# Scores of the first eight head pairs as native float32 products, two heads on 64 rows each

## The chip, the cores and the metric

The kernel runs on one core of a Trainium2 chip. The metric is the device time of one execution in microseconds (us): 705.78 us, the median of three runs (705.69 to 705.79).

## The reference, cut to what matters

```python
# q, k, v: (4, 12, 448, 64) float32; cap = 30; w_in: (768, 2048), w_out: (2048, 768) float64
scores = (1 / sqrt(64)) * matmul(q, k.transpose(0, 1, 3, 2))
scores = cap * tanh(scores / cap)
scores = scores - max(scores, axis=-1)
attn = exp(scores) / (sum(exp(scores), axis=-1) + 1e-09)
x = matmul(attn, v)              # then (4, 448, 12*64) -> (1792, 768)
h = x @ w_in
out = (h - tanh(h)) @ w_out      # (1792, 768)
```

## The kernel before, in words

Attention is worked per pair: head p and head p+6 of one batch, 24 pairs in all. Keys lie on the partitions of a score tile, in blocks of 128 (three full blocks and a tail of 64 per head; the tails of the two heads share one block), and the 448 queries lie along the free axis. A score tile goes through tanh (scale 1/(8 cap) put in beforehand), an exponential with scale cap, and then as moving operand into the product with v, which has columns of ones beside it for the sums (`pv`, L880 to L885). `numerators` and `normalize` divide. The expert layers follow: `first` (L1213 to L1215) and `second` (L1266) are products in three parts, high times high, high times low and low times high, in the one-pass type float32r; weights arrive as 64-bit floats and are decoded on VectorE (L1067 to L1081). Work of the layers for batch 0 is woven into the attention of batch 1, and so on.

The order on each engine is written out by a planner (`Plan.schedule`). Every operation is declared with an engine, an estimated cost, dependencies, buffers by tag and a due time; a list scheduler simulates all engines with these costs and fixes one order for each. "AD" operations (`copy`, L448 on ScalarE, L450 on VectorE) may go to either engine. So a changed cost or buffer changes the order of everything behind it. `SCORES` and `GROUP` are such costs.

Scores come in three kinds of work. Pairs 0 to 7 (`TILED_PAIRS`) are the tiled ones. For them `prep_pair` turns k and q with a VectorE transpose (L552), splits k into a float32r high part (a copy) and a low part (`split`, L459), copies the tails of both parts into `kt`, and makes the scaled q high on ScalarE (L575) and q low on VectorE (L580). `qk_group` (L736) then issues, for each full block, three products for each of the two heads, head 0 on rows 0 to 63 and head 1 on rows 64 to 127 of the array, the heads taken in turn: six 64-row products a group, three groups a pair. The tail block is three 128-row products with `kt`. ScalarE's tanh (L746) reads the result. Later pairs use 128-row stacks (`stack_pair`, L701) and are as they were. Pairs 0 to 10 (`F32_PAIRS`) multiply v in native float32 (L880), the others in float32r.

Of the kernel before, what the change touches and what calls it, by code (L numbers as in the profile page):

```python
# [58 lines left out]
COLS = {256: 118.0, 384: 175.5, 448: 204.0, 512: 233.0}  # L59
SCORE, FULL32 = COLS[448], 750.0  # L60

GROUP = 3 * SCORE + 400.0
SCORES = 3 * GROUP + 3 * SCORE

SHIFT = 110.0

# [248 lines left out]
class Build:  # L315
# [6 lines left out]
    def __init__(self, ctx, tc, q, k, v, w_in, w_out, out, consts, checks, general):  # L322
        self.tc, self.nc = tc, tc.nc
        nc = self.nc
        self.q, self.k, self.v, self.w_in, self.w_out, self.out = q, k, v, w_in, w_out, out
        self.general = general
        self.absc, self.s8 = consts
        self.B, self.H, self.S, self.D = q.shape
        self.NP = self.H // 2
        self.DM, self.DFF = w_in.shape  # L330
        self.ND = self.DM // 128
        self.NF = self.DFF // 128
        self.FULL = self.S // 128 * 128
        self.TAIL = self.S - self.FULL
        B, S, D = self.B, self.S, self.D
        nm = self.nm = "g" if general else "f"
        self.cst = ctx.enter_context(tc.tile_pool(name=nm + "cst", bufs=1))
        self.sb = ctx.enter_context(tc.tile_pool(name=nm + "sb", bufs=2))
        self.ps = ctx.enter_context(tc.tile_pool(name=nm + "ps", bufs=1, space=PSUM))
        self.dram = ctx.enter_context(tc.tile_pool(name=nm + "dram", bufs=1, space=bass.MemoryType.DRAM))  # L340
        self.u_kept = [self.dram.tile([128, 2, self.DM], F32, name=f"{nm}uk{f}") for f in range(self.NF)]
        self.uid = 0
        self.plan = Plan(self.make)
        for name, n in self.sizes().items():
            self.plan.tag(name, n)

        self.fixed = {"kst": [], "kz": [], "kt": [], "vraw": []}  # L350
        S = self.S
        for i in range(self.plan.tags["kst"]):
            t = self.cst.tile([128, 2 * S + self.TAIL], F32R, name=f"{nm}kst{i}")
            nc.gpsimd.memset(t.bitcast(F32)[:, S : S + self.TAIL], 0.0)
            self.fixed["kst"].append(t)


        for i in range(self.plan.tags["kz"]):
            t = self.cst.tile([128, 2 * S], F32R, name=f"{nm}kz{i}")
            nc.gpsimd.memset(t.bitcast(F32)[D:, 0:S], 0.0)  # L360
            nc.gpsimd.memset(t.bitcast(F32)[:D, S:], 0.0)
            self.fixed["kz"].append(t)
        for i in range(self.plan.tags["kt"]):
            t = self.cst.tile([128, 2, 2, self.TAIL], F32R, name=f"{nm}kt{i}")
            nc.gpsimd.memset(t.bitcast(F32)[:D, :, 1, :], 0.0)
            nc.gpsimd.memset(t.bitcast(F32)[D:, :, 0, :], 0.0)
            self.fixed["kt"].append(t)
        self.v1s = {F32: [], F32R: []}
        for i in range(self.plan.tags["vraw"]):
            t = self.cst.tile([128, 4, 2, D], F32, name=f"{nm}vraw{i}")  # L370
            self.fixed["vraw"].append(t)
        tail = B * self.TAIL
        self.xt = [self.cst.tile([128, tail], F32, name=f"{nm}xt{d}") for d in range(self.ND)]
        self.x, self.xt_ops = {}, {d: [] for d in range(self.ND)}
        self.raw_qk, self.ready, self.raw_v = {}, {}, {}
        self.raw, self.u, self.w, self.kept_op = {}, {}, {}, {}
        self.segments = [(m, a, z) for m, a, z in SEGMENTS]
        later = {m for m, a, _ in self.segments if a}
        self.x_kept = {
            m: [self.dram.tile([128, 2, self.FULL], F32, name=f"{nm}xk{m}_{d}") for d in range(self.ND)] for m in later  # L380
        }
        self.y_kept = {
            m: [self.dram.tile([128, self.DM], F32, name=f"{nm}yk{m}_{i}") for i in range(3)] for m in later
        }
        self.x_ops, self.y_ops = {}, {}
        self.acc = {}
        self.at = 0.0
        if not general:
            self.least, self.flagf, self.flag = checks
            self.seen = self.cst.tile([128, 2, self.NF], F32, name="seen")  # L390
            self.ok = self.cst.tile([128, 2, self.NF], F32, name="ok")
            self.bad = self.cst.tile([128, 2], F32, name="bad")
            self.seen_ops = []

    def sizes(self):
        g = self.general
        n = dict(kraw=2, qraw=2, kT=1, qT=1, kst=2, kz=1, ql=1, kt=1, qst=2, vraw=1, v1=3, v2=2, e=2, eh=4, el=3)
        n.update(num=1, sumT=1, r14=2, rb=1, x=self.NP, xh=self.ND, xl=self.ND, w64=2, u=2, wi=2, wo=3)
        n.update(g=1, gh=1, gl=1, o=3, s=2, h=1, acc0=1, acc1=1, acc2=1, acc3=1, acc4=1)
        if g:  # L400
# [140 lines left out]
    def prep_pair(self, b, p):  # L541

        nc, S, D, F, TL, plan = self.nc, self.S, self.D, self.FULL, self.TAIL, self.plan
        T, tr = {}, {}
        for nm in ("k", "q"):
            raw, j, ops = self.raw_qk.pop((nm, b, p))
            t = T[nm] = plan.buf(nm + "T", [128, S])
            tr[nm] = self.dve(  # L550
                S,
                lambda t=t, raw=raw, j=j: nc.vector.transpose(t(), raw()[:, j].rearrange("p j a -> p (j a)")),  # L552
                ops, [t], [raw],
            )
        if not self.tiled(b, p):
            return self.stack_pair(b, p, T, tr)
        kst, kt, qst = plan.buf("kst"), plan.buf("kt"), plan.buf("qst", [128, 2, S], F32R)
        kops = list(
            self.split(
                S, lambda: kst()[:, :S], lambda: kst()[:, S + TL :], T["k"], [tr["k"]], ([kst], []),  # L560
                ([T["k"]], [kst, T["k"]]),
            )
        )
        tops = []
        for h, c0 in ((0, F), (1, 0)):
            rows = slice(D * h, D * h + D)
            tops.append(
                self.copy(
                    2 * TL, lambda h=h, rows=rows: kt()[rows, :, h, :],
                    lambda rows=rows, c0=c0: self.pieces(kst(), rows, c0), kops,  # L570
                    [] if h else [kt], [kst, kt] if h else [kst],
                )
            )
        o1 = self.act(
            S, lambda: nc.scalar.activation(qst()[:, 0, :], T["q"](), AF.Copy, scale=self.s8), [tr["q"]],  # L575
            [qst], [T["q"]], aps=1,
        )
        o2 = self.dve(
            S,
            lambda: nc.vector.scalar_tensor_tensor(  # L580
                qst()[:, 1, :], T["q"](), self.s8, qst()[:, 0, :].bitcast(F32), op0=ALU.mult, op1=ALU.subtract
            ),
            [o1], [], [qst, T["q"]], extra=60,
        )
        self.ready[b, p] = dict(kst=kst, kt=kt, qst=qst, kops=kops, tops=tops, qops=[o1, o2])

    def tiled(self, b, p):
        return b * self.NP + p < TILED_PAIRS

    def pieces(self, kst, rows, c0):  # L590

        S, TL = self.S, self.TAIL
        t = kst[rows, c0 : c0 + S + 2 * TL].bitcast(F32)
        return t.rearrange("p (a b) -> p a b", b=TL)[:, 0 : S // TL + 2 : S // TL + 1, :]

    def stack_pair(self, b, p, T, tr):

# [113 lines left out]
        )  # L711
        return [t], cost

    PRODUCTS = ((0, 0), (0, 1), (1, 0))

    def qk_group(self, b, p, c, dsts, e):

        nc, S, D = self.nc, self.S, self.D
# [5 lines left out]
        ps = self.s_banks(b, p, heads)  # L724

        def fn():
            qst = r["qst"]()
            for n, (i, j) in enumerate(self.PRODUCTS):
                for h in range(heads):
                    rows = slice(D * h, D * h + D) if heads == 2 else slice(0, 2 * D)  # L730
                    c0 = 128 * c + self.TAIL * h
                    if heads == 2:
                        k = r["kst"]()[rows, (S + self.TAIL) * i + c0 : (S + self.TAIL) * i + c0 + 128]
                    else:
                        k = r["kt"]()[:, i].rearrange("p a b -> p (a b)")
                    nc.tensor.matmul(ps[h]()[:, :S], k, qst[rows, j, :], start=n == 0, stop=n == 2)  # L736

        cost = GROUP if heads == 2 else 3 * SCORE
        ks = "kst" if heads == 2 else "kt"
        o = self.pe(cost, fn, r["kops" if heads == 2 else "tops"] + r["qops"], ps, [r[ks], r["qst"]])  # L740
        ts = []
        for h in range(heads):
            new = e.users == 0
            ts.append(
                self.act(
                    S, lambda h=h: nc.scalar.activation(dsts[h](), ps[h]()[:, :S], AF.Tanh), [o],  # L746
                    [e] if new else [], [ps[h]] if new else [ps[h], e], psum=True, key=self.at + cost + 400,
                )
            )
        return ts, cost  # L750
# [862 lines left out]
```

## Time and profile before

| what | value |
|---|---|
| median of three runs | 705.78 us |
| the profiled execution, its own time | 704.82 us |
| its span, first to last instruction | 703.0 us |
| TensorE matmuls busy | 686.1 us (98%) |
| VectorE busy | 520.5 us (74%) |
| ScalarE busy | 535.6 us (76%) |
| mean granted TensorE clock | 0.995 |
| share of the chain that ended last | PE 70%, ACT 12%, DVE 10% |

Engines are PE (TensorE matmul), PEld (its weight loads), DVE (VectorE), ACT (ScalarE), POOL (GpSimd) and SP (the queue of most transfers). A matmul's shape is written as rows*columns of the array, then the moving operand. One native float32 product stands in the trace as two matmul records (88 products with v in float32 are 176 records at L880), a float32r product as one. All are printed as f32. Starts of matmuls are recorded; their ends are modelled and overlap the next start, so time on TensorE is read from start to start. The tiled pairs' scores run from 8.4 to 95.5 us of the span.

### The profile page before, as it was taken

Reading aid. Unit: us, or ns where it says so; the run is one execution under the profiler, and the core shown is the slowest. Engines: PE = TensorE matmul, PEld = TensorE weight load, DVE = VectorE, ACT = ScalarE, POOL = GpSimd, SP = SyncE. Lnnn points to the kernel's source line nnn. Section 1 sums busy time; section 2 is a strip of 40 time slices with the busy share of each in tenths; the row PEclk is TensorE's granted clock in tenths of the full one; section 3 lists DMA queues with packets and bytes.
Section 4 is the critical chain, followed back from the end, with each engine's and each line's share of the span. In section 5 each row is a group of like instructions: output and inputs, shape, how many; then the busy total and the mean of one; then the engine's idle time right before and its main releaser. Section 6 shows DMA issues by size and latency. Waiting matters only on the chain.

```text
span 703.0 us, 10228 instructions
## 1 busy us (share of the span) xinstructions
PE 686.1 (98%) x3672; PEld 587.7 (84%) x3672; DVE 520.5 (74%) x799; ACT 535.6 (76%) x925; POOL 21.9 (3%) x51
## 2 busy tenths in 40 slices
PE   8999999999999999999999999999999999999995
PEld 6445677777889998899989888989999999999995
DVE  4889998999887889998799789798784334333431
ACT  6988878788896959498888998899785555555454
POOL 2011100000000000000000000000000000000000
PEclk9999999999999999999999999999999999999998
DMA  7999999999954646799576865577569544566513
GB/s 107 162 226 243 280 252 243 212 238 260 192 201 147 132 133 188 262 198 323 191 162 190 259 183 149 173 202 217 156 175 269 166 126 135 159 180 179 142 39 118
DMA packets 159520, 133.06 MB, mean 189 GB/s; under 512 B 115748, under 2 KB 144036, under 8 KB 159460
## 3 DMA queue, kind: packets, MB, share of 16 engines
q1 hardware_dynamic: 156308, 117.30, 66.5%
q0 software_dynamic: 3072, 14.94, 5.9%
q8 instruction: 31, 0.51, 0.3%
q14 instruction: 29, 0.24, 0.1%
q10 hardware_dynamic: 80, 0.07, 0.0%
HBM read 110.66 MB, written 21.63 MB: 188 GB/s over the span
## 4 chain that ended last, share of the span: by engine, by line
PE 70%; ACT 12%; DVE 10%; issue 3%; DMA 2%; SPq 2%; DVEq 0%; ACTq 0%
PE facc L1266 22%; PE fh L1213 9%; PE fh L1215 9%; PE fh L1214 9%; PE fs L880 4%; PE fs L701 4%; PE fs L1266 3%; PE fs L882 3%; PE fs L883 2%; PE fs L885 2%; SPq L499 2%; DVE fu L1074 1%; DVE fsumT L912 1%; ACT fe L801 1%; ACT fe L709 1%
## 5 line engine op out<-in xcount | busy, mean ns | idle before, releaser
L1266 PE MATMUL facc<-fwo,fgh 128*128 128x512 f32 (+1 forms) x768 | 167.5, 340 | 0.0
L1266 PEld LDWEIGHTS facc<-fwo,fgh 128*128 128x128 f32 x768 | 123.8, 188 | 15.8 <-issue 2.2
L1213 PE MATMUL fh<-fxh,fwi 128*128 128x384 f32 x384 | 132.8, 346 | 1.1 <-DVE fg L1228 1.1
L1215 PE MATMUL fh<-fxh,fwi 128*128 128x384 f32 x384 | 129.9, 338 | 0.0
L1214 PE MATMUL fh<-fxl,fwi 128*128 128x384 f32 x384 | 128.7, 335 | 0.0
L1266 PE MATMUL facc<-fwo,fgl 128*128 128x512 f32 (+1 forms) x384 | 98.6, 338 | 0.0
L1228 DVE TENSOR_TENSOR fg<-fh,fg 128x384 f32<-128x384 f32 x64 | 35.6, 556 | 64.1 <-ACT fg L1226 63.5
L459 DVE TENSOR_TENSOR fwi<-fu,fwi 128x768 fp32r<-128x768 f32 x66 | 62.9, 953 | 22.3 <-ACT fwi L448 21.4
L1213 PEld LDWEIGHTS fh<-fxh,fwi 128*128 128x128 f32 x384 | 72.1, 188 | 7.0 <-DVE fg L1228 2.6
L448 ACT CAST fwi<-fu 128x768 fp32r<-128x768 f32 x59 | 49.3, 836 | 34.1 <-PE fh L1215 31.1
L1214 PEld LDWEIGHTS fh<-fxl,fwi 128*128 128x128 f32 x384 | 72.2, 188 | 2.1 <-issue 1.3
L1215 PEld LDWEIGHTS fh<-fxh,fwi 128*128 128x128 f32 x384 | 72.0, 187 | 0.0
L459 DVE TENSOR_TENSOR fwo<-fu,fwo 128x768 fp32r<-128x768 f32 x66 | 62.9, 953 | 10.0 <-ACT fwo L448 9.2
L1266 PEld LDWEIGHTS facc<-fwo,fgl 128*128 128x128 f32 x384 | 58.7, 188 | 8.4
L1226 ACT ACTIVATE fg<-fh 128x384 f32<-128x384 f32 x64 | 31.2, 488 | 35.9 <-PE fh L1215 35.6
L709 ACT ACTIVATE fe<-fs 128x448 f32<-128x448 f32 x91 | 46.8, 543 | 10.3 <-PE fs L701 9.6
L801 ACT ACTIVATE fe<-fe,absc 128x896 f32<-128x896 f32 (+1 forms) x52 | 48.8, 954 | 0.3
L448 ACT CAST fgh<-fg 128x384 fp32r<-128x384 f32 x63 | 32.5, 516 | 21.0 <-PE facc L1266 11.1
L701 PE MATMUL fs<-fqst,fkst 128*128 128x448 f32 x128 | 45.9, 379 | 2.2 <-DVE fsumT L912 1.0
L459 DVE TENSOR_TENSOR fgl<-fg,fgh 128x384 fp32r<-128x384 f32 x64 | 35.3, 552 | 15.3 <-ACT fgh L448 14.9
L459 DVE TENSOR_TENSOR fel<-fe,feh 128x896 fp32r<-128x896 f32 x39 | 42.5, 1090 | 5.1 <-ACT feh L448 4.5
L448 ACT CAST fwo<-fu 128x768 fp32r<-128x768 f32 x53 | 44.3, 836 | 1.9
(188 smaller groups left out, 1307.7 us busy)
## 6 DMA issues: line engine op xcount, KB each, us to landing
fu<-fuk SPq DMA_DIRECT2D x48, 768.0 KB
fw<-in_moe_w_in_dram SPq DMA_DIRECT2D x64, 384.0 KB
fw<-in_moe_w_out_dram SPq DMA_DIRECT2D x32, 768.0 KB
fuk<-fu POOLq DMA_DIRECT2D x16, 768.0 KB, 5.9
fqraw<-in_q_dram SPq DMA_DIRECT2D x44, 112.0 KB
fkraw<-in_k_dram SPq DMA_DIRECT2D x44, 112.0 KB
out_dram<-fo SPq DMA_DIRECT2D x12, 384.0 KB
fvraw<-in_v_dram SPq DMA_DIRECT2D x26, 96.0 KB
```

Of the source, the lines that this page charges most:

```text
L448: self.nc.scalar.copy(out(), in_())
L459: lambda: self.nc.vector.tensor_sub(lo(), x(), hi().bitcast(F32)),
L701: nc.tensor.matmul(ps()[:, :S], k, q, start=n == 0, stop=n == passes - 1)
L709: S, lambda: nc.scalar.activation(dst(), ps()[:, :S], AF.Tanh), [o],
L801: lambda e=e, w=w: nc.scalar.activation(e()[:, :w, :], e()[:, :w, :], AF.Exp, scale=self.absc),
L880: nc.tensor.matmul(out, va, e, start=n == 0, stop=n == 3)
L1213: nc.tensor.matmul(h()[:, :n], wh, ah, start=(d == 0), stop=False)
L1214: nc.tensor.matmul(h()[:, :n], wh, al, start=False, stop=False)
L1215: nc.tensor.matmul(h()[:, :n], wl, ah, start=False, stop=(d == ND - 1))
L1226: n, lambda: nc.scalar.activation(g()[:, :n], h()[:, :n], AF.Tanh), [prev], [g], [h], psum=True, key=k
L1228: o = self.dve(n, lambda: nc.vector.tensor_sub(g()[:, :n], h()[:, :n], g()[:, :n]), [o], [], [g, h], key=k + 600)
L1266: nc.tensor.matmul(banks[bk]()[:, c0 : c0 + ne], lhs()[:, ts], w()[:, k, e0 : e0 + ne], start=bk in firsts and bk not in begun, stop=stop ...
```

## The change

For the tiled pairs k and q are not split any more. `plain_pair` turns both, k into a `kT` buffer (now two of them) and q into a `qst` buffer, and copies the two tails, unsplit, to `kt`, which is now float32. `qk_group` issues one native float32 product per head and block, head 0 on rows 0 to 63 and then head 1 on rows 64 to 127, and one 128-row float32 product for the tail block. The factor 1/(8 cap) goes into the tanh as its scale operand. The planner's cost of a group goes from 3 x 204 + 400 to 750 + 450 ns, that of a tail block from 612 to 750. The new helper `turn` holds the transpose; the splitting branch and `pieces` go.

```diff
-GROUP = 3 * SCORE + 400.0
-SCORES = 3 * GROUP + 3 * SCORE
+PLAIN = FULL32 + 450.0
+SCORES = 3 * PLAIN + FULL32
...
-            t = self.cst.tile([128, 2, 2, self.TAIL], F32R, name=f"{nm}kt{i}")
...
+            t = self.cst.tile([128, 2, self.TAIL], F32, name=f"{nm}kt{i}")
...
-        n = dict(kraw=2, qraw=2, kT=1, qT=1, kst=2, ...
+        n = dict(kraw=2, qraw=2, kT=2, qT=1, kst=2, ...
...
+    def plain_pair(self, b, p):
+        S, D, F, TL, plan = self.S, self.D, self.FULL, self.TAIL, self.plan
+        k, q, kt = plan.buf("kT", [128, S]), plan.buf("qst", [128, S]), plan.buf("kt")
+        ko, qo = self.turn("k", b, p, k, k), self.turn("q", b, p, q, q)
         tops = []
         for h, c0 in ((0, F), (1, 0)):
             rows = slice(D * h, D * h + D)
             tops.append(
                 self.copy(
-                    2 * TL, lambda h=h, rows=rows: kt()[rows, :, h, :],
-                    lambda rows=rows, c0=c0: self.pieces(kst(), rows, c0), kops,
-                    [] if h else [kt], [kst, kt] if h else [kst],
+                    TL, lambda h=h, rows=rows: kt()[rows, h, :], lambda rows=rows, c0=c0: k()[rows, c0 : c0 + TL],
+                    [ko], [] if h else [kt], [k, kt] if h else [k],
                 )
             )
-        o1 = self.act(
-            S, lambda: nc.scalar.activation(qst()[:, 0, :], T["q"](), AF.Copy, scale=self.s8), [tr["q"]],
-            [qst], [T["q"]], aps=1,
-        )
-        o2 = self.dve(
...
+        self.ready[b, p] = dict(kst=k, kt=kt, qst=q, kops=[ko], tops=tops, qops=[qo])
...
-            for n, (i, j) in enumerate(self.PRODUCTS):
-                for h in range(heads):
...
-                    nc.tensor.matmul(ps[h]()[:, :S], k, qst[rows, j, :], start=n == 0, stop=n == 2)
+            for h in range(heads):
+                rows = slice(D * h, D * h + D) if heads == 2 else slice(0, 2 * D)
+                c0 = 128 * c + self.TAIL * h
+                if heads == 2:
+                    k = r["kst"]()[rows, c0 : c0 + 128]
+                else:
+                    k = r["kt"]().rearrange("p a b -> p (a b)")
+                nc.tensor.matmul(ps[h]()[:, :S], k, r["qst"]()[rows], start=True, stop=True)
...
-                    S, lambda h=h: nc.scalar.activation(dsts[h](), ps[h]()[:, :S], AF.Tanh), [o],
+                    S, lambda h=h: nc.scalar.activation(dsts[h](), ps[h]()[:, :S], AF.Tanh, scale=self.s8), [o],
```

## Rows read from the trace of the kernel before

**Rows 1.** Busy time by stretch: us, PE PEld DVE ACT POOL (xinstructions), clock, DMA, GB/s.
```profile
14.00:97.00 83.00, 80.44 (x331) 45.83 (x328) 73.28 (x122) 71.28 (x124) 9.18 (x16) 1.00 1.09 229
...
205.00:690.00 485.00, 483.42 (x2758) 442.71 (x2757) 342.34 (x519) 361.25 (x621) 3.20 (x6) 1.00 0.62 178
```

**Rows 2.** Chain of work that ended last, tiled stage: start us, us, what.
```profile
27.93 0.80 PE facc L736 x6
...
55.33 0.69 DVE fqst L580
```

**Rows 3.** Groups by line, PE: xcount | busy us, mean ns | idle us <-releasers.
```profile
L1213 PE MATMUL fh<-fxh,fwi 128*128 128x384 f32 x384 | 132.8, 346 | 1.1 <-DVE fg L1228 1.1
...
L701 PE MATMUL fs<-fqst,fkst 128*128 128x448 f32 x128 | 45.9, 379 | 2.2 <-DVE fsumT L912 1.0 <-ACT fe L709 0.5 <-ACT fnum L448 0.3
...
L736 PE MATMUL facc<-fqst,fkst 64*128 64x448 f32 x123 | 20.5, 413 | 1.6 <-ACT fkst L448 1.6
...
L736 PE MATMUL facc<-fqst,fkt 128*128 128x448 f32 x21 | 7.7, 479 | 0.0
```

**Rows 4.** Timeline of PE, 14 to 46 us: start us, us, operation, xcount.
```profile
15.09 1.66 PE L880 MATMUL fs<-fel,fv1float 128*128 128x448 f32 x4
16.59 0.92 PE L880 MATMUL fs<-feh,fv1float 128*128 128x448 f32 x2
...
27.02 0.91 PE L880 MATMUL fs<-feh,fv1float 128*128 128x448 f32 x2
27.86 0.87 PE L736 MATMUL facc<-fqst,fkst 64*128 64x448 f32 x6
28.67 1.02 PE L880 MATMUL fs<-feh,fv1float 128*128 128x448 f32 x2
29.52 1.67 PE L880 MATMUL fs<-fel,fv1float 128*128 128x448 f32 x4
...
31.93 1.77 PE L880 MATMUL fs<-feh,fv1float 128*128 128x448 f32 x4
...
34.24 0.87 PE L736 MATMUL facc<-fqst,fkst 64*128 64x448 f32 x6
```

**Rows 5.** Timeline of PE in four narrow windows of one group, 13.1 to 14.3 us.
```profile
13.13 0.46 PE L736 MATMUL facc<-fqst,fkst 64*128 64x448 f32 x1
...
13.57 0.47 PE L736 MATMUL facc<-fqst,fkst 64*128 64x448 f32 x2
...
13.88 0.37 PE L736 MATMUL facc<-fqst,fkst 64*128 64x448 f32 x2
...
14.08 0.36 PE L736 MATMUL facc<-fqst,fkst 64*128 64x448 f32 x1
```

**Rows 6.** Groups by line of DVE, 0 to 100 us.
```profile
L580 DVE SCALAR_TENSOR_TENSOR fqst<-fqT,s,fqst 128x448 fp32r<-128x448 f32 x8 | 5.4, 676 | 3.0 <-ACT fqst L575 2.8
L459 DVE TENSOR_TENSOR fkst<-fkT,fkst 128x448 fp32r<-128x448 f32 x8 | 4.9, 612 | 0.9 <-ACT fkst L448 0.6
```

**Rows 7.** Groups by line of ACT, 0 to 100 us.
```profile
L746 ACT ACTIVATE feh<-facc 128x448 f32<-128x448 f32 x26 | 13.2, 555 | 0.0
...
L801 ACT ACTIVATE fel<-fel,absc 128x448 f32<-128x448 f32 x8 | 5.5, 690 | 0.1
L575 ACT ACTIVATE fqst<-fqT,s 128x448 fp32r<-128x448 f32 x8 | 5.5, 689 | 6.9 <-DVE fqT L552 4.2 <-PE facc L736 2.7
```

**Rows 8.** Timeline of PE, 46 to 100 us: rows that begin with idle time.
```profile
65.28 0.44 PE L736 MATMUL fs<-fqst,fkst 64*128 64x448 f32 x1 [0.47 <-DVE fsumT L912]
...
75.28 0.47 PE L736 MATMUL fs<-fqst,fkst 64*128 64x448 f32 x1 [1.07 <-ACT fel L746]
...
79.02 1.77 PE L880 MATMUL fs<-fel,fv1float 128*128 128x448 f32 x4 [0.49 <-ACT feh L746]
```

**Rows 9.** Timeline of DVE and of PE at the start.
```profile
7.13 0.64 DVE L552 STREAM_TRANSPOSE fkT<-fkraw 128x448 f32<-128x448 f32 x1
...
8.42 1.24 PE L736 MATMUL facc<-fqst,fkst 64*128 64x448 f32 x6 [1.59 <-ACT fkst L448]
```

More of the change, by code (lines that the diff above doesn't have):

```diff
@@ L363, in __init__ @@
         for i in range(self.plan.tags["kt"]):
-            t = self.cst.tile([128, 2, 2, self.TAIL], F32R, name=f"{nm}kt{i}")
-            nc.gpsimd.memset(t.bitcast(F32)[:D, :, 1, :], 0.0)
-            nc.gpsimd.memset(t.bitcast(F32)[D:, :, 0, :], 0.0)
+            t = self.cst.tile([128, 2, self.TAIL], F32, name=f"{nm}kt{i}")
+            nc.gpsimd.memset(t[:D, 1, :], 0.0)
+            nc.gpsimd.memset(t[D:, 0, :], 0.0)
             self.fixed["kt"].append(t)
@@ L396, in sizes @@
         g = self.general
-        n = dict(kraw=2, qraw=2, kT=1, qT=1, kst=2, kz=1, ql=1, kt=1, qst=2, vraw=1, v1=3, v2=2, e=2, eh=4, el=3)
+        n = dict(kraw=2, qraw=2, kT=2, qT=1, kst=2, kz=1, ql=1, kt=1, qst=2, vraw=1, v1=3, v2=2, e=2, eh=4, el=3)
         n.update(num=1, sumT=1, r14=2, rb=1, x=self.NP, xh=self.ND, xl=self.ND, w64=2, u=2, wi=2, wo=3)
@@ L545, in prep_pair, with turn @@
         nc, S, D, F, TL, plan = self.nc, self.S, self.D, self.FULL, self.TAIL, self.plan
+        if self.tiled(b, p):
+            return self.plain_pair(b, p)
         T, tr = {}, {}
         for nm in ("k", "q"):
-            raw, j, ops = self.raw_qk.pop((nm, b, p))
             t = T[nm] = plan.buf(nm + "T", [128, S])
[L550 to L553, printed above, removed]
-            )
[L555 to L562, printed above, removed]
-        )
+            tr[nm] = self.turn(nm, b, p, t, t)
+        self.stack_pair(b, p, T, tr)
+    def turn(self, nm, b, p, t, at):
+        raw, j, ops = self.raw_qk.pop((nm, b, p))
+        return self.dve(
+            self.S, lambda: self.nc.vector.transpose(at(), raw()[:, j].rearrange("p j a -> p (j a)")), ops, [t], [raw]
+        )
+    def plain_pair(self, b, p):
+        S, D, F, TL, plan = self.S, self.D, self.FULL, self.TAIL, self.plan
+        k, q, kt = plan.buf("kT", [128, S]), plan.buf("qst", [128, S]), plan.buf("kt")
+        ko, qo = self.turn("k", b, p, k, k), self.turn("q", b, p, q, q)
         tops = []
@@ L568, in prep_pair @@
                 self.copy(
-                    2 * TL, lambda h=h, rows=rows: kt()[rows, :, h, :],
-                    lambda rows=rows, c0=c0: self.pieces(kst(), rows, c0), kops,
-                    [] if h else [kt], [kst, kt] if h else [kst],
-                )
-            )
-        o1 = self.act(
-            S, lambda: nc.scalar.activation(qst()[:, 0, :], T["q"](), AF.Copy, scale=self.s8), [tr["q"]],
-            [qst], [T["q"]], aps=1,
-        )
-        o2 = self.dve(
[L579 to L585, printed above, removed]
+                    TL, lambda h=h, rows=rows: kt()[rows, h, :], lambda rows=rows, c0=c0: k()[rows, c0 : c0 + TL],
+                    [ko], [] if h else [kt], [k, kt] if h else [k],
+                )
+            )
+        self.ready[b, p] = dict(kst=k, kt=kt, qst=q, kops=[ko], tops=tops, qops=[qo])
     def tiled(self, b, p):
         return b * self.NP + p < TILED_PAIRS
[L590 to L594, printed above, removed]
     def stack_pair(self, b, p, T, tr):
@@ L712, in stacked_block @@
         return [t], cost
-    PRODUCTS = ((0, 0), (0, 1), (1, 0))
     def qk_group(self, b, p, c, dsts, e):
@@ L726, in fn @@
         def fn():
-            qst = r["qst"]()
-            for n, (i, j) in enumerate(self.PRODUCTS):
-                for h in range(heads):
[L730 to L735, printed above, removed]
-                    nc.tensor.matmul(ps[h]()[:, :S], k, qst[rows, j, :], start=n == 0, stop=n == 2)
-        cost = GROUP if heads == 2 else 3 * SCORE
+            for h in range(heads):
[6 more added lines that the diff above has]
+                nc.tensor.matmul(ps[h]()[:, :S], k, r["qst"]()[rows], start=True, stop=True)
+        cost = PLAIN if heads == 2 else FULL32
         ks = "kst" if heads == 2 else "kt"
@@ L745, in qk_group @@
                 self.act(
-                    S, lambda h=h: nc.scalar.activation(dsts[h](), ps[h]()[:, :S], AF.Tanh), [o],
-                    [e] if new else [], [ps[h]] if new else [ps[h], e], psum=True, key=self.at + cost + 400,
+                    S, lambda h=h: nc.scalar.activation(dsts[h](), ps[h]()[:, :S], AF.Tanh, scale=self.s8), [o],
+                    [e] if new else [], [ps[h]] if new else [ps[h], e], psum=True, aps=1, key=self.at + cost + 400,
                 )
```

## The prediction

> **What bounds the kernel now.** I read the busy time by stretch first. From 205 to 690 us TensorE's matmuls cover 483.4 of 485 us [rows 1]: whatever reaches that part later ends later by as much. From 14 to 97 us, where the eight tiled pairs' scores run, TensorE covers 80.4 of 83 us, VectorE 73.3 and ScalarE 71.3 [rows 1]. So TensorE is the bound there too, with VectorE and ScalarE close behind. The chain of waits shows both: pieces of TensorE (the six-product score groups among them) alternate with VectorE pieces such as the low part of q [rows 2]. The groups by line then say how little TensorE waits at all: in the stacked scores 2.2 us and in the first layer 1.1 us over the whole span [rows 3], and in the tiled stage three waits of 0.47, 1.07 and 0.49 us behind VectorE and ScalarE [rows 8]. Hence my account: new time = old time + TensorE work added - TensorE waits recovered. What VectorE and ScalarE save counts only through those waits.
>
> **TensorE, the score groups.** There are 24 groups (123 records of `facc` at L736 and 21 more of `fs`, six a group) [rows 3]. First today's price, from the timeline. Float32 records that follow each other without a switch start 0.375 us apart (four in 16.59 - 15.09) [rows 4]. The two records from 27.02 are through at 27.02 + 2 x 0.375 = 27.77, yet the group starts at 27.86: 0.09 us are lost on entry. The two records behind it take 29.52 - 28.67 = 0.85 instead of 0.75: 0.10 lost on leaving. The group thus costs 28.67 + 0.10 - 27.77 = 1.00 us [rows 4]. Of this the products are 3 x 0.207: the tail block, which ends a float32 run without a change of rows, lasts from 31.93 + 0.10 + 4 x 0.375 = 33.53 to 34.24, less 0.09 of entry for the group behind it, so 0.62 for three products [rows 4]. Two heads at a time take the time of one. The other 0.38 us of a group is what changing between 128 and 64 rows costs; it stays.
>
> After the change a group is two products, each of two records of 0.375, since a native product on 64 rows streams the same 448 queries. The trace before has no 64-row float32 product, so I bound it. Below: both heads fully side by side, 0.75 + 0.38 = 1.13 us. Above: one after the other, 1.50 + 0.38 = 1.88 us. Between them lies the order of issue. Today the heads alternate record by record; now head 0's two records both come before head 1's. One group in the trace shows what TensorE does when the heads fall out of step: head 0's first product starts alone at 13.13, head 1's first is held up, and head 0's second, whose row half had been free for some 0.13 us (a first product takes 13.88 - 13.57 = 0.31 us there), starts only at 13.57, together with head 1's first; then pairs at 13.57 and 13.88 and one alone at 14.08 [rows 5]. Four steps instead of three: a record ahead in the queue holds those behind it, and the two row halves do overlap once their records stand side by side. With the new order this gives head 0 first, then head 0 second beside head 1 first, then head 1 second: three steps, 3 x 0.375 + 0.38 = 1.51 us. I take 1.51, because rows 5 are the nearest thing to it: +0.51 us a group, 24 x 0.51 = +12.1 us (at the ends +3.1 and +21.1).
>
> The Trainium skill ("TensorE: Matmul & The Clock Gate", Part 3: Packing small matmuls) has two rules on this that point to different ends. By its span model tiles packed on different rows take the time of one product and some 4 ns more, which would be the lower bound. By its list of what overlaps, matmuls start and end strictly in program order and only weight loads are pulled forward, which would be the staggered price. Rows 5 agree with the second; no row here shows the first for a product of two records.
>
> **TensorE, the tail blocks.** Eight, 0.62 us today, one native 128-row product of 0.75 after: +0.13 each, +1.0 us. TensorE work in all: +13.1 us (+4.1 to +22.1).
>
> **VectorE.** Gone: eight low parts of q at 676 ns and eight low parts of k at 612 ns, 10.3 us [rows 6], besides the first copies of k and half the width of the tails' copies, which either engine may do and which I leave out. Ten microseconds off 73.3 busy of 83 [rows 1] make VectorE free enough to be late nowhere in this stage; that is what can recover the waits of rows 8.
>
> **ScalarE.** Gone: eight scalings of q at 689 ns, 5.5 us [rows 7]. Added: a scale operand on 56 tanh (seven a pair). No row has this tanh; below, it costs nothing; above, as much as the difference of the two 448-wide activations with such an operand (690 and 689 ns) to the tanh without (555 ns), 0.135 us, 7.6 us in all [rows 7]. Part of that difference is the source (the tanh reads a PSUM bank), so I take 0.09, 5.0 us. ScalarE is then level (-5.5 to +2.1), hidden under TensorE; were the cover gone, the upper end would cost 2 us. Each tanh ends up to 0.135 us later, in a chain where the product with v is issued a group or more behind its scores, so it adds no wait.
>
> **Start.** The first group starts at 8.42, released by the copy of k [rows 9]. After the change it needs only the transpose, which ends at 7.13 + 0.64 = 7.77. TensorE starts 0.6 us earlier.
>
> **Queues, buffers, planner.** No transfer is added. k is now held in `kT` until its products are done, as it was in `kst`, and there are two of each: no new wait. The planner reckons 1.20 us for a group; if it takes 1.51, TensorE is up to 24 x 0.31 = 7 us later than planned by the end of the stage, and what waits for it waits on engines with room. A new order also moves waits elsewhere; of the 3.3 us of later waits [rows 3] I count 1.0 as recovered, since decoding gets ahead of a later TensorE, and keep zero and 3.3 as ends.
>
> **Sum.** +13.1 work - 0.6 start - 2.0 waits in the stage - 1.0 later = +9.5 us. From the profiled execution's own 704.8 us (span 703.0 and 1.8 around it) this is 714.3; the median of the runs lies 1.0 above that execution, so the forecast is 715.3 us.
>
> **Rivals.**
> - *Fully side by side.* The two heads' records do not hold each other; a group costs 1.13. For: overlap of row halves is plain in the groups today. Against: the late start of rows 5. +4.1 - 3.6 = +0.5 from the median: 706.3 us.
> - *Faster: the waits decide.* With the work of VectorE and ScalarE gone, all waits behind them go: 0.6 at the start, 2.0 in the stage and 3.3 later, 5.9 us in all. Less 1.0 for the tail blocks this pays for 24 groups of up to 1.00 + 4.9/24 = 1.20 us; so it decides only if a group stays under 1.20. At 1.13: +4.1 - 5.9 = -1.8, 704.0 us. For: the VectorE pieces on the chain [rows 2]. Against: the later waits lie in stages with a full VectorE of their own.
> - *No overlap.* Native products on two row halves run one after the other, so the change does not do what it says: 1.88 a group, +22.1 - 3.6 = +18.5, 724.3 us. For: no row shows two float32 products at once. Against: the row halves overlap for the one-pass type.
>
> **How the numbers follow.** Staggered 0.54, 715.3 us (711 to 719 with its own waits); fully side by side 0.20; faster by the waits 0.10; no overlap 0.16. A measurement of this kernel can tell about 0.2%, 1.4 us, from no change. The faster case (0.10) and the low edge of the side-by-side case (0.02) give 0.12 for faster by more; most of the side-by-side case lies within 0.2% or just above: 0.12 same; 0.76 slower. The range goes from 704.5 (the side-by-side case and a little of the faster) to 722 (the lower part of no overlap): about 0.08 is left out below and 0.11 above.
>
> **What would show it.** In the timeline of the changed kernel a group is four 64-row records: three distinct starts 0.375 us apart, the middle one double, mean staggered; two double starts mean side by side; four single starts mean no overlap. Start to start around a group 1.3 (1.51 less what rows 4 show as loss outside it) against 0.80 today. TensorE's waits in rows 8 should be gone, L580 and L575 vanish, and VectorE's busy time up to about 100 us fall by 10 us or more. The end of the tiled stage should move out by about 10 us and the part behind 205 us keep its length. The prediction is wrong if a group stays under 1.2 us, or if the stage grows and the end does not.

## The result, and the profile after

The changed kernel takes 712.57 us, the median of eight runs (708.69 to 714.96); the kernel before, on the same chip, 705.57 us (704.42 to 706.08). The ratio is 1.0093, with a 95% interval from 1.0071 to 1.0115: 7.0 us slower by the medians, 6.6 by the ratio. The runs of the changed kernel spread over 6.3 us, those of the kernel before over 1.7 us. The profiled execution took 713.31 us, its span 711.5 us, 8.5 us more than before.

First the page: span, busy time of TensorE, and the granted clock in 40 slices of 17.8 us.

```profile
span 711.5 us, 10089 instructions
...
PE 695.0 (98%) x3616; PEld 583.2 (82%) x3616; DVE 504.3 (71%) x777; ACT 532.9 (75%) x915; POOL 22.2 (3%) x51
...
PEclk9999799999999999999999999999999999999999
```

VectorE went from 520.5 to 504.3 us, TensorE from 686.1 to 695.0. One slice, the fifth, has a lower clock. Busy time by stretch of the changed kernel (columns as in [rows 1]):

```profile
70.00:80.00 10.00, 6.19 (x15) 2.87 (x15) 6.04 (x10) 3.22 (x6) 1.61 (x3) 0.85 0.86 190
80.00:90.00 10.00, 10.00 (x26) 4.32 (x23) 6.34 (x15) 7.24 (x12) 1.08 (x2) 0.64 1.05 289
...
77.00:78.43 1.43, 0.00 (x1) 0.00 (x1) 1.40 (x3) 1.38 (x3) 0.32 (x1) 0.50 0.87 327
...
14.00:97.00 83.00, 79.19 (x240) 36.60 (x239) 59.16 (x93) 67.48 (x113) 9.63 (x16) 0.94 1.02 222
97.00:205.00 108.00, 106.66 (x505) 85.23 (x504) 97.71 (x142) 87.13 (x152) 4.80 (x9) 1.00 0.97 227
205.00:690.00 485.00, 482.71 (x2733) 439.98 (x2732) 336.63 (x513) 362.50 (x625) 3.20 (x6) 1.00 0.63 179
```

Behind 205 us TensorE is idle for 2.3 us against 1.6 [rows 1]: nearly all that was lost was lost ahead of that. VectorE has 14 us less to do between 14 and 97 us, and TensorE waits more there all the same. The timeline of TensorE in the changed kernel, the groups in narrow windows (a row's records may go on behind its window; columns as in [rows 4]; in brackets the idle time before the row and what ended it):

```profile
7.68 0.99 PE L716 MATMUL facc<-fqst,fkt 128*128 128x448 f32 x2 [1.12 <-DVE fqst L558]
...
12.00 0.99 PE L716 MATMUL facc<-fqst,fkt 128*128 128x448 f32 x2 [0.37 <-DVE fqst L558]
...
12.92 0.64 PE L716 MATMUL facc<-fqst,fkT 64*128 64x448 f32 x1
...
13.26 0.68 PE L716 MATMUL facc<-fqst,fkT 64*128 64x448 f32 x2
13.74 0.54 PE L716 MATMUL facc<-fqst,fkT 64*128 64x448 f32 x1
...
16.66 0.65 PE L716 MATMUL facc<-fqst,fkT 64*128 64x448 f32 x2
17.14 0.54 PE L716 MATMUL facc<-fqst,fkT 64*128 64x448 f32 x2
17.61 1.02 PE L860 MATMUL fs<-feh,fv1float 128*128 128x448 f32 x2
...
43.05 0.92 PE L716 MATMUL facc<-fqst,fkt 128*128 128x448 f32 x2
...
53.27 0.92 PE L716 MATMUL facc<-fqst,fkt 128*128 128x448 f32 x2
...
78.43 1.11 PE L716 MATMUL fs<-fqst,fkT 64*128 64x448 f32 x1 [3.81 <-DVE fsumT L892]
```

A group is two double starts, 16.66 and 17.14, and the next product starts at 17.61: the two heads run side by side. Start to start that is 0.95 us against 0.80 before, and with the same 0.20 us around it as in [rows 4] a group costs 1.15 us against 1.00. A whole pair (tail block to tail block, with the same sixteen products of v between) takes 53.27 - 43.05 = 10.22 us. In the kernel before, by the same view, it took 9.63:

```profile
42.84 1.12 PE L736 MATMUL facc<-fqst,fkt 128*128 128x448 f32 x3
...
52.47 1.12 PE L736 MATMUL facc<-fqst,fkt 128*128 128x448 f32 x3
```

So the products cost 0.59 us a pair more (three groups at 0.15, the tail block 0.14), 8 x 0.59 = +4.7 us in all. To this come the wait of 3.81 us that ends at 78.43, a new one of 0.37 us ahead of 12.00, and the clock that fell in the long wait: the windows from 70 to 90 us have 0.15 and 0.36 less than the full clock, 10 x 0.51 = 5.1 us. Of these 0.7 lie in the wait itself (half the clock from 77.00 to 78.43, with TensorE idle) and cost nothing more, so the clock takes 4.4. That is +13.3. Against it stand the earlier start (0.7), a lower clock that the kernel before had in its first 20 us and the changed one has not (0.96 and 0.86 by tens, 1.8 us), and the waits of the kernel before in this stage, all gone (0.20, 0.32 and the three of [rows 8], 2.6 us). The sum is +8.2; 8.5 were seen. It is a rough sum: work that is added where TensorE waits anyway, as at the start, need not show in full. The chain of waits of the changed kernel says where that wait came from (start us, us, what; SPq is SyncE's queue issuing a transfer):

```profile
66.52 0.29 SPq L526
...
66.86 2.35 SPq L528
...
69.90 3.75 DMA fqraw<-in_q_dram
...
73.67 0.65 DVE fqT L558
74.31 1.65 DVE fu L1061
...
75.99 0.84 ACT fwo L448
...
76.85 0.96 DVE fwo L459
77.81 0.57 DVE fsumT L892
...
78.43 1.80 PE fs L716 x2
```

Read it upwards. TensorE needs a PSUM bank that the transpose of the sums (`fsumT`) has to empty. That transpose stands on VectorE behind a transpose of q (`fqT`), whose last piece was issued behind transfers of v (L526, L528) and landed at 73.64. In the kernel before, the two waits on VectorE in this stage were 0.32 and 0.47 us long.

### The profile page after: what moved, and what is told of

It reads as the page before. It is cut to its first block, busy times and chain, and to the rows that moved or that the text cites. A ratio compares the mean times of both kernels' runs of the same rounds, so it can differ in the third digit from the quotient of the medians.

```text
span 711.5 us, 10089 instructions
## 1 busy us (share of the span) xinstructions
PE 695.0 (98%) x3616; PEld 583.2 (82%) x3616; DVE 504.3 (71%) x777; ACT 532.9 (75%) x915; POOL 22.2 (3%) x51
## 4 chain that ended last, share of the span: by engine, by line
PE 73%; ACT 13%; DVE 6%; SPq 3%; issue 2%; DMA 2%; ACTq 0%; DVEq 0%
PE facc L1246 21%; PE fh L1193 9%; PE fh L1195 9%; PE fh L1194 9%; PE fs L860 8%; PE fs L685 4%; PE fs L1246 3%; PE facc L716 3%; SPq L499 2%; PE fs L862 2%; PE fs L863 2%; ACT fe L781 2%; ACT fe L693 1%; PE fs L865 1%; ACT feh L448 1%
## 5 line engine op out<-in xcount | busy, mean ns | idle before, releaser
L1246 PEld LDWEIGHTS facc<-fwo,fgh 128*128 128x128 f32 x768 | 125.5, 188 | 17.1 <-issue 2.3
L448 ACT CAST fwo<-fu 128x768 fp32r<-128x768 f32 x51 | 42.4, 832 | 5.2 <-DVE fu L1061 5.2
```

Of the source, the lines that this page charges most:

```text
L448: self.nc.scalar.copy(out(), in_())
L1246: nc.tensor.matmul(banks[bk]()[:, c0 : c0 + ne], lhs()[:, ts], w()[:, k, e0 : e0 + ne], start=bk in firsts and bk not in begun, stop=stop ...
```

## The experiments

Each kernel was timed against the kernel before on the same chip; ratios are to that one, with 95% intervals, and differences in us are those of the medians where nothing else is said. The theory at the start: the groups cost little, and the one wait behind the late q, with its half clock, makes the rest. The rival: the written order as a whole, which the planner made anew, meets its waits at many places.

### One instruction of the order moved behind the sums

```diff
+        turns = [i for i, (o, e) in enumerate(order) if e == "D" and [b.tag for b in o.uses] == ["qT", "qraw"]]
...
+            sums = [i for i, (o, e) in enumerate(order) if i > at and e == "D" and {b.tag for b in o.uses} == {"sumT", "s"}]
+            order.insert(sums[1], order.pop(at))
```

> The changed kernel, with one VectorE instruction moved in the written order: the transpose of q for the first stacked pair (the one that waits 3.42 us for its transfer at 70 us) goes behind the two sum transposes that follow it. Nothing else is moved. Theory: that late transfer holds VectorE's queue, the sum transposes behind it hold the PSUM bank, and TensorE's wait of 3.81 us at 74.5 us comes from this, with the half clock of some 3.4 us that follows it; so the wait shrinks under 1.5 us, the granted clock stays full between 78 and 84 us, and the time falls from about 712.6 to 707 to 709.5 us. Rival: the transfers are behind anyway and the next instruction that needs one holds the same queue, or ScalarE's cast behind the decode does; then the wait stays over 2.5 us and the time within 711 to 714.

710.73 us (709.42 to 716.12), ratio 1.0087 [1.0056, 1.0118]. The profiled execution has a span of 708.8 us. Its timeline of TensorE (two idle rows and the last of the 24 groups), and its stretch from 97 to 205 us:

```profile
78.35 1.02 PE L722 MATMUL fs<-fqst,fkT 64*128 64x448 f32 x2 [0.23 <-ACT feh L732]
...
97.15 1.02 PE L722 MATMUL fs<-fqst,fkT 64*128 64x448 f32 x4
...
150.92 0.47 PE L691 MATMUL fs<-fqst,fkst 128*128 128x448 f32 x1 [1.22 <-DVE fsumT L898]
```

```profile
97.00:205.00 108.00, 103.62 (x481) 80.61 (x480) 95.56 (x141) 87.28 (x153) 4.79 (x9) 1.00 0.93 219
```

The last group in the kernel before:

```profile
94.95 0.88 PE L736 MATMUL fs<-fqst,fkst 64*128 64x448 f32 x6
```

The wait is gone, the clock stays at its upper level, and the intervals of the two kernels overlap: the time did not come back and stayed above the 707 to 709.5 us of the theory. (The half clock that went with the wait had lasted from 77.0 to 87.2 us, 10.2 us and not the 3.4 of the expectation.) TensorE is short of 4.4 us between 97 and 205 us instead, against 1.3 in the changed kernel and 2.0 in the kernel before. So the wait at 78 us is what the chain says it is, but taking it away doesn't bring the 7 us back. Where this execution loses is plain all the same: its last group starts 2.2 us later than that of the kernel before, while its span is 5.8 us longer (708.8 against 703.0). So 3.6 us are lost behind the last changed product, among operations that the change left as they were; 2.4 of them are idle time of TensorE between 97 and 205 us, and the rest isn't located. The single times say the same of the clock: of two executions of the changed kernel with a mean granted clock of 0.996, one took 708.69 us, the other 714.96.

### The heads in turn, with the products of before

```diff
-            for n, (i, j) in enumerate(self.PRODUCTS):
-                for h in range(heads):
+            for h in range(heads):
+                for n, (i, j) in enumerate(self.PRODUCTS):
```

> The kernel before, with the six one-pass products of a group issued head 0 first (three products), then head 1 (three), instead of head by head in turn. Theory (the two row halves are served independently, a busy half does not hold the queue): a group keeps its three steps and 1.00 us, six records in three double starts, time within 1 us of the kernel before. Rival (the prediction's step: a record ahead in the queue holds those behind it): head 0 first, head 0 second, head 0 third beside head 1 first, then two more, five steps, 5 x 0.207 + 0.38 = 1.42 us a group, +10 us, 713 to 717 us.

708.23 us (706.08 to 709.09), ratio 1.0032 [1.0018, 1.0045]. Its timeline of TensorE in narrow windows of one group:

```profile
28.08 0.47 PE L736 MATMUL facc<-fqst,fkst 64*128 64x448 f32 x2
28.38 0.37 PE L736 MATMUL facc<-fqst,fkst 64*128 64x448 f32 x2
28.59 0.37 PE L736 MATMUL facc<-fqst,fkst 64*128 64x448 f32 x2
28.89 0.64 PE L880 MATMUL fs<-feh,fv1float 128*128 128x448 f32 x1
```

Three double starts, and the next product 0.81 us behind the first, as before. Head 1's first product, fourth in the queue, starts with head 0's first: the three of head 0 don't hold it. That refutes the step of the prediction that did, if TensorE's queue has them in the order in which the kernel issues them, which the trace doesn't print. What held the second record back in [rows 5] stands in another row of the kernel before, that of the weight load of head 1's first product (PEld, in a narrow window):

```profile
13.57 0.18 PEld L736 LDWEIGHTS facc<-fqst,fkst 64*128 64x128 f32 x1 [0.25 <-ACT fel L746]
```

It waited for ScalarE's tanh, which reads the scores out of their bank. The median of the heads in turn is 2.7 us higher all the same, with no group changed, outside what either side expected; the profiled execution, at 706.08 us the shortest of the ten, shows little of it (one wait at 79.59 of 1.25 us, where [rows 8] has 0.49). Six of the ten runs have a mean granted clock of 0.990 to 0.992, which none of the 29 runs of the kernel before has (0.994 to 0.998), and these six take 707.9 to 708.6 us. Why their clock fell stays open, since no trace was kept of them.

### The scale alone

The kernel before with the factor taken out of q and put into the tanh; k and q still split.

```diff
-            S, lambda: nc.scalar.activation(qst()[:, 0, :], T["q"](), AF.Copy, scale=self.s8), [tr["q"]],
...
-                    S, lambda h=h: nc.scalar.activation(dsts[h](), ps[h]()[:, :S], AF.Tanh), [o],
+                    S, lambda h=h: nc.scalar.activation(dsts[h](), ps[h]()[:, :S], AF.Tanh, scale=self.s8), [o],
```

> The kernel before with the scale part alone: k and q are split as before into two one-pass parts and the products are the six of before, but q is split unscaled (a plain copy and a subtraction) and the tanh takes the scale operand. Theory: ScalarE gains and loses about the same (56 tanh by about 0.09 us, +5 us, against eight scalings, -5.5 us, of which some come back as plain copies), hidden under TensorE: within 1.5 us of the kernel before. Rival: in the tiled stage ScalarE is close enough to the bound that the longer tanh delays the scores' banks: 2 to 5 us slower than before.

705.42 us (704.98 to 706.39), ratio 0.9996 [0.9987, 1.0005]. Its tanh, by groups of ScalarE up to 100 us:

```profile
L741 ACT ACTIVATE feh<-facc,s 128x448 f32<-128x448 f32 x26 | 15.1, 630 | 0.2
```

630 ns against 555 [rows 7]: +0.075 us each, paid in full on ScalarE and not seen in the time.

### The change for the first two pairs, and for the first six

k and q of these pairs lie unsplit in the two halves of one `qst` buffer; the other tiled pairs are as before.

```diff
+PLAIN, PLAIN_PAIRS = FULL32 + 450.0, 2
...
+    def plain(self, b, p):
+        return b * self.NP + p < PLAIN_PAIRS
```

> The kernel before, with the change made for the first two pairs alone (unsplit k and q, float32 products, scale in the tanh); the other six tiled pairs as before. Theory: the start gains what the changed kernel's trace shows there (first product 7.7 against 8.4 us, first product with v at 14.2 against 15.1, no half clock between 9 and 13 us) and the six extra groups cost 6 x 0.15 + 2 x 0.13 = 1.2 us: 704 to 705.5 us. Rival: what the start gains is lost again at the next pair, whose transfers are no earlier, and the new order costs about as much: 705.5 to 707.5 us.

> The kernel before, with the change for the first six pairs (batch 0) and the one-pass products for the last two tiled pairs, which run beside the expert layers. Added TensorE work 18 x 0.15 + 6 x 0.13 = 3.5 us, 0.6 us and half a clock window gained at the start. Theory (the loss beyond the work arises where the tiled pairs meet the layers, at 70 us and later): 706.5 to 708.5 us. Rival (the loss grows with the number of changed pairs alike): about three quarters of the changed kernel's, 710 to 711.5 us.

With two pairs 705.98 us (703.98 to 707.60), ratio 0.9998 [0.9985, 1.0011]: the earlier start buys nothing that can be measured. With six 710.22 us (710.04 to 713.77), ratio 1.0074 [1.0054, 1.0093]: 4.6 us for products that cost 6 x 0.59 = 3.5, which is what the rival expected. Its longest wait lies in neither place seen so far:

```profile
48.29 1.79 PE L930 MATMUL fs<-fel,fv1float 128*128 128x448 f32 x2 [2.61 <-DVE fsumT L962]
```

### The planner told that transfers are late

If the loss comes from q arriving later than the planner reckoned, telling it so should help. The same edit was made to the changed kernel and, as a control, to the kernel before.

```diff
-                    self.dma("SP", np_ * S * 128, fn, [], [] if ops else [raw], [raw] if ops else [], slow=2.3)
+                    self.dma(
+                        "SP", np_ * S * 128, fn, [], [] if ops else [raw], [raw] if ops else [], slow=2.3,
+                        lag=3000.0 if (b, p) > (0, 1) else 0.0,
+                    )
```

> The changed kernel, with the planner told that the transfers of k and q from the third pair on land 3 us later than it reckons (a lag as the transfers of weights and v have already); the work is the same, the written order differs. Theory: the changed kernel's waits between 70 and 210 us come from an order that puts instructions which need late transfers ahead of others; with room for them the TensorE waits shrink and only the added TensorE work is left: 707 to 709.5 us, with less spread between runs. Rival: the waits come from the transfers' own rate or from full engines, and another order only moves them: 710 to 714 us.

> Control: the kernel before, with the same 3 us of lag in the planner for k and q. Theory: its order already fits the transfers as they are, so the lag gives nothing or costs the waits of a less dense plan: 705 to 708 us. Rival: the lag alone makes any order faster by a microsecond or more, under 704.5; then a gain of the run with the lag in the changed kernel says nothing about the change.

The changed kernel so edited takes 711.64 us (709.97 to 715.22), ratio 1.0078 [1.0062, 1.0094]; its profiled execution, the longest of the six, waits longest far behind the stage:

```profile
196.30 0.74 PE L688 MATMUL fs<-fqst,fkst 128*128 128x448 f32 x1 [4.48 <-DVE fsumT L895]
```

The control takes 710.05 us (708.64 to 711.39), ratio 1.0058 [1.0041, 1.0075], outside both bands that were expected. It is the most telling run: not one operation is added or taken away, only the written order differs from the kernel before, and with it the engine of about ten copies that may go to either, and that costs 4.4 us. Its idle rows of TensorE:

```profile
24.60 0.99 PE L883 MATMUL fs<-fel,fv1float 128*128 128x448 f32 x2 [1.49 <-issue]
47.00 0.99 PE L883 MATMUL fs<-fel,fv1float 128*128 128x448 f32 x2 [1.46 <-issue]
...
77.43 0.47 PE L739 MATMUL fs<-fqst,fkst 64*128 64x448 f32 x1 [1.72 <-DVE fsumT L915]
80.64 1.49 PE L739 MATMUL facc<-fqst,fkt 128*128 128x448 f32 x3 [1.65 <-ACT fel L749]
```

Four waits of about 1.5 us, in places where the kernel before has waits of 0.20 to 1.07 us or none. Part of the price is the clock, which fell with these waits: its mean is 0.989 to 0.993 in the six runs, against 0.994 to 0.998 in the kernel before.

### The six products of each group twice

The kernel before in its own order; the second set starts afresh.

```diff
-            for n, (i, j) in enumerate(self.PRODUCTS):
+            for n, (i, j) in enumerate(self.PRODUCTS + self.PRODUCTS if heads == 2 else self.PRODUCTS):
...
-                    nc.tensor.matmul(ps[h]()[:, :S], k, qst[rows, j, :], start=n == 0, stop=n == 2)
+                        ps[h]()[:, :S], k, qst[rows, j, :], start=n % 3 == 0, stop=n % 3 == 2
```

> The kernel before, with the six products of each of the 24 groups issued twice over (the second set gives the result), nothing else changed, the planner not told. Adds 24 x 3 x 0.207 = 14.9 us of TensorE work in the tiled stage. Theory (TensorE is the bound there and its work passes one for one): +13 to +15 us less up to 2 us of waits that it swallows, 717 to 721 us. Rival (TensorE has hidden room in this stage): under +10 us.

714.65 us (714.35 to 714.99), ratio 1.0127 [1.0110, 1.0144]: +9.0 us. A group in its timeline:

```profile
17.99 1.49 PE L736 MATMUL facc<-fqst,fkst 64*128 64x448 f32 x12
19.41 1.02 PE L882 MATMUL fs<-feh,fv1float 128*128 128x448 f32 x2
```

Start to start 1.42 us, 0.62 more than in the kernel before, so 24 x 0.62 = 14.9 us were added and 5.9 of them don't show in the end. When the order stays as it is, work added to the bounding engine shows only in part in the time. That 5.9 is also the sum of all waits that the prediction listed (0.6 + 2.0 + 3.3) proves nothing: in the profiled executions TensorE's time without work (span less busy time) fell by only 2.2 us, from 16.9 to 14.7, and two waits of [rows 8] are still there, with 0.36 and 1.07 us. The half clock at the start of the kernel before (1.8 us) is absent here; the rest isn't located.

### The native products alone, in the old order

The operations and the order of the kernel before, but a group is two float32 products of the high parts, and the low parts are computed and not used; then also without computing them (the last two lines of the diff, for k and for q, are the second kernel's alone).

```diff
-            qst = r["qst"]()
-            for n, (i, j) in enumerate(self.PRODUCTS):
+            qst = r["qst"]().bitcast(F32)
+            for n, (i, j) in enumerate(self.PRODUCTS[:1]):
...
+        self.plan.ops[-1].fn = lambda: None
...
+        o2.fn = lambda: None
```

> The kernel before with the products alone changed: float32 products, two heads on 64 rows each, and one for the tail, of the high parts of k and q (the low parts are still computed and are left out of the sum). All work of VectorE and ScalarE and the written order of every engine are those of the kernel before; the planner is not told. Added TensorE work 24 x 0.15 + 8 x 0.13 = 4.6 us. Theory (most of what the change loses is its new written order, and TensorE work in this stage is partly swallowed by waits, 14.9 us having cost 9): 705.5 to 709 us. Rival (the products themselves cost it): 710 to 714 us.

> As the run with the products alone, and the low parts of k and q are not computed either (left out: their two VectorE instructions a pair and half of the tails' copies), so VectorE does 10 us less, as in the changed kernel; the written order is still that of the kernel before, and the scale stays in q. Theory: with the order kept, the freed VectorE gives back up to 2 us of the waits between 64 and 80 us: 704 to 707.5 us, at or under the run with the products alone. Rival: a VectorE that runs ahead only waits for transfers sooner and the time is the same as with the products alone; second rival, the changed kernel's loss comes with the work and shows here too: 710 us or more.

With the low parts 706.49 us (705.87 to 707.07), ratio 1.0018 [1.0009, 1.0027]. Without them 705.72 us (705.46 to 707.21), ratio 1.0007 [0.9998, 1.0017]. The first one's timeline of TensorE, a pair and a group:

```profile
44.11 0.92 PE L736 MATMUL facc<-fqst,fkt 128*128 128x448 f32 x2
44.96 1.02 PE L736 MATMUL facc<-fqst,fkst 64*128 64x448 f32 x4
45.91 1.02 PE L880 MATMUL fs<-fel,fv1float 128*128 128x448 f32 x2
...
54.33 0.92 PE L736 MATMUL facc<-fqst,fkt 128*128 128x448 f32 x2
...
66.87 0.61 PE L736 MATMUL fs<-fqst,fkst 64*128 64x448 f32 x1 [0.28 <-DVE fsumT L912]
...
77.17 0.64 PE L736 MATMUL fs<-fqst,fkst 64*128 64x448 f32 x1 [1.06 <-ACT fel L746]
...
96.81 1.02 PE L736 MATMUL fs<-fqst,fkst 64*128 64x448 f32 x4
```

And of the second, without the low parts:

```profile
77.84 0.64 PE L738 MATMUL fs<-fqst,fkst 64*128 64x448 f32 x1 [1.06 <-ACT fel L748]
```

The products are those of the changed kernel, to the hundredth: a pair of 10.22 us, a group of 0.95 start to start. In the old order they cost 1.3 us by the ratio (1.0 by the medians), and 0.5 (-0.1 to 1.2; 0.3 by the medians) with VectorE relieved as well. This is the change without its new order, and it lies where the side-by-side rival put the time (706.3 us).

### The planner's old costs for the new products

The changed kernel with the costs of a group and of a tail block put back.

```diff
-PLAIN = FULL32 + 450.0
-SCORES = 3 * PLAIN + FULL32
+PLAIN = 3 * SCORE + 400.0
+SCORES = 3 * PLAIN + 3 * SCORE
```

> The changed kernel with the planner's costs of a group and of a tail block put back to those of the kernel before (1012 and 612 ns): the work is that of the changed kernel, the written order is another one. Theory (the order decides by some microseconds, whatever the work): the time differs from 712.6 by more than 1.5 us, on either side, with other TensorE waits than those at 74 us. Rival (the work decides): 711.5 to 713.5 us.

709.04 us (707.49 to 714.71), ratio 1.0063 [1.0038, 1.0088]. Idle rows of its TensorE:

```profile
75.51 1.32 PE L716 MATMUL fs<-fqst,fkT 64*128 64x448 f32 x3 [2.05 <-DVE fsumT L892]
...
183.25 0.44 PE L862 MATMUL fs<-feh,fv1float32r 128*128 128x448 f32 x1 [1.94 <-ACT fe L693]
```

A third order for the same work, with its waits elsewhere again and a median between; its interval overlaps that of the changed kernel.

## Why the prediction was right or wrong, point by point

The time came out 2.7 us under the forecast of 715.3, and on the side forecast, but by luck: two errors nearly cancel, 8.5 us too many for the groups and some 5 to 6 us for the new order that the sum hadn't.

- **Score groups: wrong.** The step that failed is "a record ahead in the queue holds those behind it", which made a group 1.51 us. It is 1.15: the fully side-by-side case, 0.02 above its 1.13, and under the 1.2 us that the prediction itself named as the sign of being wrong. The mechanism was read out of [rows 5], a group in which head 1's first product came late. The changed kernel has such a group too: starts at 12.920, 13.261, 13.400 and 13.741. A head's second record follows its first by 0.48 us, as in 16.66 and 17.14, so head 0 has 12.920 and 13.400, head 1 the other two, and neither waits for the other. The heads in turn show the same from the other side. In rows 5 the weight load of head 1's first product waited 0.25 us for ScalarE's tanh; the reading that fits is that, as an instruction that waits, it kept the next one, head 0's second, behind it. A busy row half doesn't do that. The 24 groups thus cost 3.6 us instead of 12.1.
- The span model of the Trainium skill ("TensorE: Matmul & The Clock Gate", Part 3: Packing small matmuls), one product's time and about 4 ns more for a second tile, agrees with the double starts here, which lie 7 ns apart (16.659 and 16.666). Its statement in the same part that matmuls start strictly in program order does not: in the run with the heads in turn the fourth that the kernel issues starts with the first, and the measurement decides.
- **Tail blocks: right.** +0.14 each against +0.13.
- **The account (work added less waits recovered): its number fits a kept order, the waits that it names don't.** With the measured +4.7 it gives 4.7 - 3.6 = +1.1; the products alone measured +1.3 (0.6 to 1.9). Doubling the products went the same way over a wider stretch: 14.9 added, 9.0 paid. But the waits that were to pay are mostly still there: of [rows 8] the products alone keep 0.28 of 0.47 us and 1.06 of 1.07. In their profiled execution the last group starts 1.9 us later than before (96.81 against 94.95) for 4.6 us of work added ahead of it. The waits of 0.20 and 0.32 us are gone, and the clock gave up to 1.8 us back: from 10 to 20 us it was 1.00, where the kernel before had 0.86. So the sum came out partly by luck.
- **VectorE and ScalarE: the work right, its worth not.** From 14 to 97 us VectorE lost 14 us of work, part of it moved. That this recovers the waits of rows 8 (2.0 us) is not borne out: relieving VectorE in the old order is worth at most about 1 us (1.3 against 0.5, with intervals that overlap), and the wait of 1.06 us at 77.84 is as long without the low parts as with them. The tanh became 0.075 us longer (0.09 taken), without effect.
- **Start: right in place, without worth.** TensorE starts at 7.68 instead of 8.42; two changed pairs alone gave nothing.
- **Queues, buffers, planner: wrong, and it decided the time.** "A new order also moves waits elsewhere" was priced only as a recovery, 0 to 3.3 us; that it could lose was given no term. Of the 7.0 us, the products in the old order make 1.0 to 1.3; 5 to 6 us are left for the new order. That an order alone can cost several us is shown (the control, +4.4 us with every operation kept), and with the long wait taken away 3.6 us are lost behind the last changed product. That the order is what costs the changed kernel the rest is argued by exclusion and not shown: products, relief and scale, each in the old order or alone, leave no more than about 1 us. The second `kT` buffer and the dropped scaling of q on ScalarE weren't run by themselves, and the changed kernel's operations, which are another list, weren't run in the order of before.
- The sentence that TensorE's waits of rows 8 "should be gone" is half right: they are gone, and one of 3.81 us stands in their stead. The end of the stage moved out as forecast, by 9.1 us (last group at 104.01 against 94.95), but by this wait and its clock more than by the groups.

Open is why nearly every new order is worse. In five of the new orders (the changed kernel, the six pairs, both with late transfers, the old costs) the longest wait of TensorE ends on the transpose of the sums. In the changed kernel this was traced to a late q, but telling the planner of late transfers helped neither kernel. Open are also the spread of 6.3 us between runs of the changed kernel and the clock in the longer runs of the heads in turn. No kernel with native products in all eight pairs beat the one before; the nearest, without low parts, is not told apart from it.

## What to carry to other kernels

Where a planner writes the order, a change has two prices: that of its operations, and that of a new order. Measure the first with the old order kept, and give the second a range with both signs, as wide as a control shows that only re-orders (here 4.4 us, more than the products cost in the old order). A start that comes late in the trace is no proof of a busy unit: look first at whether the instruction ahead of it in the queue was waiting. And when a chain names one long wait, take that wait away before it is called the cause.

## What the runs showed of the hardware that was not expected

- Two native float32 products of 448 columns on the two row halves take the time of one: 0.95 us start to start for both together, records of two double starts 0.48 us apart.
- In the run of the heads in turn the two row halves started together, at 28.08 us, though one head's three products were issued ahead of the other's. In [rows 5] an instruction that waited 0.25 us for ScalarE seems to have kept a later one of the other half back; this is a reading of one group, not tested.
- In the wait of 3.81 us TensorE's granted clock fell from 2.4 to 1.2 GHz and stayed there for some 10 us, until 87.2 us, though TensorE was busy from 78.43 us on.
